# First round of a routed expert layer: W1 products by 128-token tiles, transposes by row halves, search copies later

## The chip, the cores and the metric

The kernel runs on one core of a Trainium2 chip. The metric is the device time of one execution in microseconds (us). Engines are named as in the profile: PE is TensorE's matmul, PEld its weight load, DVE is VectorE, ACT is ScalarE, POOL is GpSimd, SP is SyncE. "L1369" is line 1369 of the kernel.

## What is computed

The first part is windowed attention over 8 batches of 8 heads, 576 positions and 64 columns; its rows become `x`, 4608 tokens of 512 columns. The second part routes the tokens to 8 experts and is where the change lies:

```python
logits = x @ w_gate
order = np.argsort(-logits.flatten())
for idx in order:
    tok, e = (int(idx) // E, int(idx) % E)
    if assigned[tok] >= 0 or counts[e] >= cap:   # cap = 4608 / 8 = 576
        continue
    assigned[tok] = e
    counts[e] += 1
for e in range(E):
    mask = assigned == e
    h = np.maximum(x[mask] @ w1[e], 0.0)
    out[mask] = h @ w2[e]
```

Each expert takes 576 tokens; `w1[e]` is 512 x 1024 and `w2[e]` is 1024 x 512.

## The kernel before, in words

Attention (L273 to L720) writes its rows to `xd` in device memory and leaves the gate's logits on the chip. The experts are then filled one after the other in eight rounds; a round is one expert. `R.alone()` (L858) searches the threshold of the first full expert with nothing beside it, and its list of tokens is made by `settle` (L1219) and `listing` (L1250).

**A round's data.** `gather` (L1276) fetches the 576 token rows with five indirect DMAs (L1283, POOL), four tiles of 128 tokens and one of 64 (`MSZ`). PE turns them (transposes against an identity), ACT rounds the turned rows to `XH` (type float32r, L1149 through `act`) and DVE keeps the rest in `XL` (L1150 through `sub`), both in `split` (L1309). In the first round (r = 0) `gather` itself turns one tile at a time, four transposes of 128 x 128 for a tile, into a bank of `PYR` (two banks, `py`) or `PTR` (one, `ptx`) (L1296 to L1305). In later rounds `turn_halves` (L1317) turns all five tiles in one go, each by its two 64-row halves, into `PHR`'s banks (`ph`, L1338).

**A round's products.** `expert` (L1352) has eight blocks f of 128 hidden columns. `first(f, j)` (L1356) makes block f for half j of the tokens: j = 0 is columns 0 to 256 (tiles 0 and 1), j = 1 is columns 256 to 576 (tiles 2, 3 and 4). Each is 12 products (L1369): four row blocks d, times w1h with XH, w1l with XH, and w1h with XL. The stationary operand is a 128 x 128 block of weights, the moving one 256 or 320 token columns. The result goes through ACT (relu to `hb`) and DVE (the rest, L1389), and then its bank is free; `PHR[j]` has two banks for each j. The order of (f, j) is (0,0), (1,0), (0,1), (1,1), (2,0), (2,1), and so on; `gemm` (L1348) makes each group of products depend on the one before it, so that order is fixed. W2's products follow (L1411, L1414, L1416), then rows go out by indirect DMA (L1437).

**The search for the next expert** runs beside the products: `close`, `leave` and `start` on DVE, then `copies` on ACT (L854, `ohr`, the flags repeated for PE), then eight steps of `counts` on PE (nine small products, L724) and `step` on DVE (L761 to L771, L738).

**What sets the order.** [...] A planner written in the kernel, `Schedule` (L156), simulates all engines with a cost in ns for each operation and due times (the longest remaining path, less a boost), and emits the instructions of each engine in that order. The planner takes a product of n columns to cost n/2.4 + 13.5 ns (L1381), and a turn of the first round 460 ns. Where the plan leaves PE idle ahead of a turn, it puts in products of zeros into the bank `PHR[0].tiles[1]` (`keep_clock`, L120) to hold the clock. [...]

Of the kernel before, what the change touches and what calls it, by code (L numbers as in the profile page):

```python
# [1116 lines left out]
def moe(tc, ctx, C, R, xd, w1, w2, out):  # L1117
# [35 lines left out]
    def weights(n, r, f, deps):  # L1153

        raw, old, use = RAW[n].take()
        if n == "1" and r < len(AHEAD_W) and f == AHEAD_W[r]:

            gate[r] = op("POOL", 100, lambda: nc.gpsimd.memset(raw[:1, :1], 0.0), [got[r, 1], *old], B_G)
        later = None
        if r in gate:  # L1160
            deps = [*deps, gate[r]]
            later = X[r][-2][0] if n == "1" and r else None

        def load():
            if n == "1":
                src = w1[bass.ds(E[r], 1), f].rearrange("o p d f -> p (o d f)")
            else:
                src = w2[bass.ds(E[r], 1), f * 128:f * 128 + 128, :].rearrange("o p d -> p (o d)")
            nc.sync.dma_start(raw, src)

        ld = op("SP", 60, load, [*deps, *old], dma=T_W)
        h, oldh, useh = WH[n].take()
        l, oldl, usel = WL[n].take()
        hi = op("ACT", 525, lambda: act(h, raw), [ld, *oldh, st["row"] if n == "1" and r == 0 else None, later], B_W)
        if (n, r) in ADDED:
            use.append(hi)
            ne = op("ACT", 525, lambda: nc.scalar.activation(l, h.bitcast(F32), AF.Copy, scale=-1.0), [hi, *oldl], B_W)
            useh.append(ne)
            lo = op("POOL", 1040, lambda: nc.gpsimd.dma_start(l, raw, accum_op=OP.add), [ne], B_W, lat=T_A if (n, r) != ADDED[2] else 500,
                    dma=T_AM if (n, r) != ADDED[2] else T_GM)  # L1180
            use.append(lo)
        else:
            lo = op("DVE", 600, lambda: sub(nc.vector, l, raw, h), [ld, hi, *oldl, st["ix"] if n == "1" and r == 0 else None], B_W)
            use += [hi, lo]
        useh.append(lo)
        return h, l, hi, lo, useh, usel
# [32 lines left out]
    def settle(r, e):  # L1219

        if r == 0:
            rk = nd = None
        elif r < NE - 1:
            nd = st["need"] = chain("DVE", 1180, R.members, [e], B_L)
            rk = chain("PE", 70, R.ranks, [nd], B_L)
        else:
            nd = chain("DVE", 400, R.rest, [e, st["left"], st["slots"]], B_L)
            rk = chain("PE", 70, R.ranks, [nd], B_L)

        def accept():  # L1230
            if r:
                R.before()
            R.accept()

        ac = chain("DVE", 730 if r else 200, accept, [rk, nd], B_L)
        sl = st["slots"] = chain("DVE", 400, lambda: R.slots(r == 0), [ac, st.get("digits")], B_L)
        ix, box = listing(r, sl)
        st["ix"] = ix
        st["left"] = None
        if r == NE - 2:  # L1240
            st["left"] = chain("DVE", 400, R.assign, [ac])
        elif r < NE - 1:
            cl = chain("DVE", 1780, R.close, [nd, ix if r == 0 else None])
            lv = chain("DVE", 1050, R.leave, [cl, ac])
            oc = chain("ACT", 1055, lambda: R.copies(R.oh, nc.scalar), [lv])
            gf = chain("DVE", 670, R.start, [cl])
            st["next"] = [oc, gf]
        return ix, box

    def listing(r, sl):  # L1250
# [25 lines left out]
    def gather(r, ix, box):  # L1276

        done, gs = [], []
        for m, n in enumerate(MSZ):
            xg, old, use = XG.take()  # L1280

            def get(xg=xg, n=n, m=m):
                nc.gpsimd.indirect_dma_start(out=xg[:n], out_offset=None, in_=xd,  # L1283
                                             in_offset=bass.IndirectOffsetOnAxis(ap=box[0][:n, m:m + 1], axis=0))

            g = op("POOL", 1040 if r else 1500, get, [ix, *old], B_G,
                   lat=2500 if r <= DENSE else T_GL if r == NE - 2 else T_G, dma=T_GM if 0 < r <= DENSE else 0)
            got[r, m] = g
            gs.append((g, xg, use))
        if r:  # L1290
            turn_halves(r, gs, done)
            return done
        for m, n in enumerate(MSZ):
            g, xg, use = gs[m]
            pt, old, usep = (PYR if m % 3 < 2 else PTR).take()
            pt = pt.rearrange("p (d x) -> p d x", d=ND)[:, :, :n]  # L1296

            def turn(pt=pt, xg=xg, n=n):
                for d in range(ND):
                    nc.tensor.transpose(pt[:, d], xg[:n, 128 * d:128 * d + 128], C["identf"][:n, :n])  # L1300

            t = op("PE", 460 if n == 128 else 250, turn, [g, *old], B_TR)
            use.append(t)
            turns.append(t)
            at = slice(128 * m, 128 * m + n)  # L1305
            split(r, m, n, t, pt, XH[:, :, at], XL[:, :, at], usep, done)
        return done

    def split(r, m, n, t, pt, a, b, use, done):  # L1309
        full = 500 if n == 128 else 290  # L1310
        wx = x_users.get((r - 1, 0 if m < 2 else 1), [])
        s0 = op("ACT", full, lambda: act(a, pt), [t, *wx], B_TR)
        s1 = op("DVE", full + 100, lambda: sub(nc.vector, b, pt, a), [s0], B_TR)
        use += [s0, s1]
        done.append((s0, s1))

    def turn_halves(r, gs, done):  # L1317

# [29 lines left out]
    def gemm(cost, fn, deps):  # L1348
        last[0] = op("PE", cost, fn, [*deps, last[0]])
        return last[0]  # L1350

    def expert(r, X, box, W1, W2):  # L1352

        hidden = {}

        def first(f, j):  # L1356
            ph, old, use = PHR[j].take()
            h, l, hi, lo, useh, usel = W1[f]
            c0, c1 = CUT[j:j + 2]
            o = ph[:, :c1 - c0]  # L1360
            xs = X[:2] if j == 0 else X[2:]
            pairs = [(d, i) for d in range(ND) for i in range(3)]
            if f < 2:
                pairs = [(d, i) for i in range(3) for d in range(ND)]

            def mm(ps_):
                for d, i in ps_:
                    a, b = ((h, XH), (l, XH), (h, XL))[i]
                    nc.tensor.matmul(o, a[:, d * 128:d * 128 + 128], b[:, d, c0:c1],  # L1369
                                     start=((d, i) == pairs[0]), stop=((d, i) == pairs[-1]))  # L1370

            n = ND if f < 2 else 3
            for k in range(0, 3 * ND, n):
                part = pairs[k:k + n]
                deps = [hi, *old] if k == 0 else []
                if any(i == 1 for _, i in part):
                    deps.append(lo)
                deps += [x[0] for x in xs] if k == 0 else []
                if any(i == 2 for _, i in part):
                    deps += [x[1] for x in xs]  # L1380
                g = gemm(n * ((c1 - c0) / 2.4 + 13.5), lambda part=part: mm(part), deps)  # L1381
            useh.append(g)
            usel.append(g)
            x_users.setdefault((r, j), []).append(g)
            if j == 0:
                hidden[f] = [*HB.take(), []]
            hb, oldh, useb, done = hidden[f]
            hh = op("ACT", 270 if j == 0 else 320, lambda: act(hb[:, c0:c1], o, AF.Relu), [g, *(oldh if j == 0 else ())], B_H)
            hl = op("DVE", 335 if j == 0 else 400, lambda: nc.vector.scalar_tensor_tensor(  # L1389
                hb[:, CAP + c0:CAP + c1], o, 0.0, hb[:, c0:c1], op0=OP.max, op1=OP.subtract), [hh], B_HL)  # L1390
            use += [hh, hl]
            done.append(hl)
            if j == 1:
                h2 = op("ACT", 190, lambda: act(hb[:, 2 * CAP:], o[:, c1 - c0 - 64:], AF.Relu), [g], B_H)
                use.append(h2)
                done.append(h2)

        for f, j in ((0, 0), (1, 0), (0, 1), (1, 1), *((f, j) for f in range(2, NF) for j in range(2))):
            first(f, j)
        gemm1_end[r] = last[0]  # L1400
        for m, n in sorted(enumerate(MSZ), key=lambda x: x[1] if r == NE - 1 else 0):
# [50 lines left out]
    def round_(r):  # L1452
        e = None
        if r:
            e = search(r) if r < NE - 1 else chain("DVE", 650, R.last, [st["fetch"], st["need"]])
        en = st["fetch"] = EN[r] = op("SP", 100, lambda: fetch(r, R.eidx), [e])
        ix, BOX[r] = settle(r, e)
        toks[r] = st["tok"]
        X[r] = gather(r, ix, BOX[r])
        W[r] = [weights("1", r, f, [en]) for f in range(NF)]  # L1460

    def first_gather():
# [92 lines left out]
```

## Time and profile before

| | |
|---|---|
| Time, median of 3 runs | 631.48 us (631.08 to 631.92) |
| The profiled execution's own time | 631.08 us |
| Its span in the profile | 629.2 us |
| PE busy | 604.9 us (96%) |
| PEld busy | 529.0 us (84%) |
| DVE, ACT, POOL busy | 443.6, 304.1, 197.4 us |
| First gather's turn of the first round begins | 174.60 us |
| First product of the first round begins | 177.48 us |

A PE busy share says that some matmul was in flight, not that the array was full; the ends of matmuls are modelled. The pace of a stream of products is read better from when they start. Weight loads run beside the products, one ahead.

### The profile page before, as it was taken

How to read it: one execution, taken by the hardware profiler on the slowest of the kernel's cores; microseconds unless marked ns; L12 is line 12 of the kernel's file. 1: busy time of each engine (PE TensorE's matmuls, PEld its weight loads, DVE VectorE, ACT ScalarE, POOL GpSimd, SP SyncE). 2: the span in 40 equal slices, each digit the busy share in tenths (PEclk: the TensorE clock that was granted, in tenths of full speed). 3: DMA queues.
4: the chain of work that ended last, by engine and by line, in shares of the span. 5: the costliest groups of instructions: out<-in, count | busy, mean ns of one | idle time of the engine just before them, and what ended most of it. 6: DMA issues, size and time to landing. Idle time of an engine off the chain costs nothing.

```text
span 629.2 us, 17943 instructions
## 1 busy us (share of the span) xinstructions
PE 604.9 (96%) x6749; PEld 529.0 (84%) x6750; DVE 443.6 (71%) x1896; ACT 304.1 (48%) x695; POOL 197.4 (31%) x331
## 2 busy tenths in 40 slices
PE   8999999896599999999999999999999999999996
PEld 5888888786379879978998898799889879988985
DVE  4778879777887878777986988698889826714200
ACT  4787788671167238744252434435343345324211
POOL 3643434330253175352025104300610520341011
PEclk9999999997599999999999999999999999999999
DMA  8989999852187279972073136116423744122001
GB/s 313 394 252 300 287 269 316 279 119 60 55 272 154 84 164 288 239 241 85 9 253 109 59 106 220 68 28 211 133 76 102 246 161 147 40 71 76 1 26 51
DMA packets 62679, 100.11 MB, mean 159 GB/s; under 512 B 7280, under 2 KB 26224, under 8 KB 62592
## 3 DMA queue, kind: packets, MB, share of 16 engines
q1 hardware_dynamic: 53216, 73.75, 36.2%
q0 software_dynamic: 9376, 25.21, 15.4%
q8 instruction: 53, 0.87, 0.6%
q14 instruction: 34, 0.28, 0.1%
HBM read 73.77 MB, written 18.87 MB: 147 GB/s over the span
## 4 chain that ended last, share of the span: by engine, by line
PE 59%; issue 12%; DVE 7%; POOL 3%; DMA 1%; POOLq 0%; ACT 0%; SPq 0%; DVEq 0%
PE ph L1369 26%; PE py L1411 19%; PE pz L724 2%; PE py L1414 2%; PE py L1416 2%; PE px L426 1%; POOL out L1437 1%; PE px L418 1%; PE ph L1338 1%; DVE ob L1072 1%; PE pm L400 1%; POOL xg L1283 1%; PE pz L798 1%; DMA raw<-in_moe_w 1%; PE px L477 1%
## 5 line engine op out<-in xcount | busy, mean ns | idle before, releaser
L1411 PE MATMUL py<-w2h,hb 128*128 128x512 f32 x512 | 165.0, 394 | 0.0
L1369 PE MATMUL ph<-xh,w1h 128*128 128x256 f32 (+1 forms) x512 | 138.4, 301 | 0.0
L1369 PE MATMUL ph<-xh,w1l 128*128 128x256 f32 (+1 forms) x512 | 136.6, 297 | 0.0
L1369 PE MATMUL ph<-xl,w1h 128*128 128x256 f32 (+1 forms) x512 | 135.9, 296 | 0.0
L1411 PEld LDWEIGHTS py<-w2h,hb 128*128 128x128 f32 x512 | 96.1, 188 | 19.7
L1149 ACT ACTIVATE hb<-ph 128x256 fp32r<-128x256 f32 (+2 forms) x192 | 59.7, 346 | 100.9 <-PE ph L1369 99.1
L1411 PE MATMUL py<-w2l,hb 128*128 128x512 f32 x256 | 99.8, 390 | 0.0
L1369 PEld LDWEIGHTS ph<-xh,w1h 128*128 128x128 f32 x512 | 91.8, 190 | 0.7
L1369 PEld LDWEIGHTS ph<-xl,w1h 128*128 128x128 f32 x512 | 91.6, 189 | 0.1
L1369 PEld LDWEIGHTS ph<-xh,w1l 128*128 128x128 f32 x512 | 91.5, 190 | 0.0
L1437 POOL DMA_INDIRECT out<-y,tok x40 | 40.6, 1015 | 144.6 <-ACT y L1149 65.3
L1149 ACT ACTIVATE y<-py 128x512 f32<-128x512 f32 (+1 forms) x40 | 23.9, 596 | 121.0 <-PE py L1411 85.7
L411 POOL TENSOR_TENSOR sc<-sc,mx 128x480 f32<-128x480 f32 x64 | 56.9, 909 | 78.4 <-DVE mx L405 78.3
L1389 DVE SCALAR_TENSOR_TENSOR hb<-ph,hb 128x320 fp32r<-128x320 f32 (+1 forms) x128 | 57.3, 452 | 33.1 <-ACT hb L1149 32.0
L405 DVE CUSTOM_DVE_ANT_0 sc<-pm,const 128x96 f32<-128x96 f32 x288 | 53.6, 252 | 17.6 <-PE pm L400 17.3
L1283 POOL DMA_INDIRECT xg<-xd,idx x40 | 41.6, 1039 | 55.8 <-issue 38.0
L1411 PEld LDWEIGHTS py<-w2l,hb 128*128 128x128 f32 x256 | 48.1, 188 | 9.1
L1150 DVE TENSOR_TENSOR w2l<-raw,w2h 128x512 fp32r<-128x512 f32 x48 | 31.9, 685 | 20.4 <-ACT w2h L1149 20.1
L414 ACT ACTIVATE et<-px 96x384 f32<-96x384 f32 x96 | 40.2, 488 | 12.5 <-PE px L418 10.4
L1149 ACT ACTIVATE w1h<-raw 128x512 fp32r<-128x512 f32 x64 | 37.8, 628 | 9.3 <-DMA raw<-in_moe_w 9.2
L418 PE MATMUL px<-const,sc 128*96 128x128 f32 x288 | 38.6, 277 | 2.2 <-issue 1.5
L1149 ACT ACTIVATE w2h<-raw 128x512 fp32r<-128x512 f32 x64 | 36.8, 622 | 3.0 <-DMA raw<-in_moe_w 3.0
(206 smaller groups left out, 967.6 us busy)
## 6 DMA issues: line engine op xcount, KB each, us to landing
raw<-in_moe_w SPq DMA_DIRECT2D x128, 256.0 KB, 4.0
k<-in_kp SPq DMA_DIRECT2D x16, 304.0 KB, 5.8
k<-in_kd SPq DMA_DIRECT2D x16, 304.0 KB, 6.8
q<-in_qp SPq DMA_DIRECT2D x16, 288.0 KB, 5.7
q<-in_qd SPq DMA_DIRECT2D x16, 288.0 KB, 6.6
xd<-xs SPq DMA_DIRECT2D x64, 72.0 KB, 2.8
xd<-xs SPq DMA_DIRECT2D x16, 288.0 KB, 5.6
w2l<-raw POOLq DMA_DIRECT2D x16, 256.0 KB
```

The lines of the kernel that those rows point to most:

```text
L405: nc.vector.tensor_tensor_reduce(out=sc[:, c], in0=pms[g][:, c // 2 * KB:c // 2 * KB + KB], in1=mm[:, c if self.kind else min(1, c)], scal ...
L411: nc.gpsimd.tensor_tensor(sc[:, g::2], sc[:, g::2], mx[:, g::2, None].to_broadcast([128, n, KB]), op=OP.subtract)
L414: nc.scalar.activation(self.E0[:, 384 * j:384 * j + 384], pt[:KB, :384], AF.Exp, scale=-1.0)
L418: nc.tensor.transpose(pt[:KB, 128 * x:128 * x + 128], sc[:, ORD[3 * j + x]], C["identf"])
L724: nc.tensor.matmul(o, self.ohr[:, j].rearrange("p r x -> p (r x)"), self.G[:, 4 * j:4 * j + 4, :w], start=(j == 0), stop=(j == NCH // 4 - 1))
L1149: act = lambda o, i, f=AF.Copy: nc.scalar.activation(o, i, f)
L1150: sub = lambda e, o, a, b: e.tensor_tensor(o, a, b, op=OP.subtract)
L1283: nc.gpsimd.indirect_dma_start(out=xg[:n], out_offset=None, in_=xd, in_offset=bass.IndirectOffsetOnAxis(ap=box[0][:n, m:m + 1], axis=0))
L1369: nc.tensor.matmul(o, a[:, d * 128:d * 128 + 128], b[:, d, c0:c1], start=((d, i) == pairs[0]), stop=((d, i) == pairs[-1]))
L1389: hl = op("DVE", 335 if j == 0 else 400, lambda: nc.vector.scalar_tensor_tensor(hb[:, CAP + c0:CAP + c1], o, 0.0, hb[:, c0:c1], op0=OP.max ...
L1411: nc.tensor.matmul(py, x, w, start=(f + i == 0), stop=(f == NF - 1 and i == 2))
L1437: s = nc.gpsimd.indirect_dma_start(out=out, out_offset=bass.IndirectOffsetOnAxis(ap=box[1][:n, m:m + 1], axis=0), in_=y[:n], in_offset=None)
```

## The change

It does three things, all in the first round (r = 0).

First, `first` is split into `products` (one group of products of block f, a range of token columns), `keep` (what follows once a bank is complete) and `by_tile`. In the first round the blocks f = 0 and f = 1 of half j = 0 are made by `by_tile`: for tile 0 and then for tile 1, the three kinds of product for f = 0 and f = 1 in turn, each a group of four products with 128 moving columns. The order then goes on with (2,0), (0,1), (1,1), (2,1).

Second, the turning of the first round moves to `turn_each`: a tile of 128 tokens is turned by its two 64-row halves into two banks (`PHR[1]` for odd tiles, `PYR` for even ones), each half split on its own; the fifth tile uses `PTR`. The planner's costs are 300 for such a turn and 330 for a half's split.

Third, `copies` of the first search waits for tile 1's two roundings.

```diff
-            oc = chain("ACT", 1055, lambda: R.copies(R.oh, nc.scalar), [lv])
+            if r == 0:
+                st["leave"] = lv
+            else:
+                oc = chain("ACT", 1055, lambda: R.copies(R.oh, nc.scalar), [lv])
             gf = chain("DVE", 670, R.start, [cl])
-            st["next"] = [oc, gf]
+            st["next"] = [oc, gf] if r else [gf]
...
+    def turn_each(r, gs, done):
         for m, n in enumerate(MSZ):
             g, xg, use = gs[m]
-            pt, old, usep = (PYR if m % 3 < 2 else PTR).take()
-            pt = pt.rearrange("p (d x) -> p d x", d=ND)[:, :, :n]
+            ring_ = PHR[1] if m % 2 else PYR
+            got_ = [ring_.take() for _ in range(2)] if n == 128 else [PTR.take()]
+            old = [y for x in got_ for y in x[1]]
+            halves = [x[0][:, :64 * ND].rearrange("p (d y) -> p d y", d=ND) for x in got_]
...
                 for d in range(ND):
-                    nc.tensor.transpose(pt[:, d], xg[:n, 128 * d:128 * d + 128], C["identf"][:n, :n])
-            t = op("PE", 460 if n == 128 else 250, turn, [g, *old], B_TR)
+                    for h, o in enumerate(halves):
+                        p = slice(64 * h, 64 * h + 64)
+                        nc.tensor.transpose(o[:, d], xg[p, 128 * d:128 * d + 128], C["identf"][p, p])
+            t = op("PE", 300, turn, [g, *old, *turns[-1:]], B_TR)
...
+            for h, (o, x) in enumerate(zip(halves, got_)):
+                p = slice(at.start + 64 * h, at.start + 64 * h + 64)
+                split(r, m, 64, t, o, XH[:, :, p], XL[:, :, p], x[2], parts)
...
-        full = 500 if n == 128 else 290
+        full = 500 if n == 128 else 290 if r or m == 4 else 330
...
+        def products(f, j, c0, c1, xs, part, open_):
...
+            return gemm(len(part) * ((c1 - c0) / 2.4 + 13.5), mm, deps)
...
+        def by_tile():
+            for m in range(2):
+                for i in range(3):
+                    for f in range(2):
+                        g = products(f, 0, 128 * m, 128 * m + 128, X[m:m + 1], [(d, i) for d in range(ND)], (i == 0, i == 2))
+                        if m and i == 2:
+                            keep(f, 0, g)
...
-        for f, j in ((0, 0), (1, 0), (0, 1), (1, 1), *((f, j) for f in range(2, NF) for j in range(2))):
+        if r == 0:
+            by_tile()
+            order = [(2, 0), (0, 1), (1, 1), (2, 1)]
+        else:
+            order = [(0, 0), (1, 0), (0, 1), (1, 1), (2, 0), (2, 1)]
+        for f, j in order + [(f, j) for f in range(3, NF) for j in range(2)]:
             first(f, j)
...
+        if r == 0:
+            st["next"].insert(0, chain("ACT", 1055, lambda: R.copies(R.oh, nc.scalar), [st["leave"], *X[r][1][0]]))
```

## Rows read from the trace of the kernel before

**Rows 1.** Busy us per engine from 182.2 to 624 us; then granted clock, DMA share, GB/s

```profile
182.20:624.00 441.80, 440.61 (x3221) 391.36 (x3217) 306.27 (x987) 187.78 (x426) 126.98 (x230) 1.00 0.42 127
```

**Rows 2.** The same by stretches of 10 us: PE, PEld, DVE, ACT, POOL

```profile
170.00:180.00 10.00, 8.84 (x51) 5.13 (x51) 8.54 (x27) 3.79 (x7) 7.40 (x14) 0.84 0.55 161
180.00:190.00 10.00, 10.00 (x82) 9.70 (x81) 8.84 (x25) 7.84 (x20) 2.88 (x7) 1.00 0.97 299
```

**Rows 3.** Timeline of PE alone, two later stalls: start, us, ..., [idle before]

```profile
226.14 0.45 PE L724 MATMUL pz<-G,ohr 128*128 128x64 bf16 x9 [0.24 <-DVE G L736]
...
268.63 0.24 PE L1079 MATMUL ptx<-rx,ob 128*128 128x40 bf16 x3 [0.62 <-DVE ob L1072]
```

**Rows 4.** Timeline of the first round's start: start, us, engine, line, [idle before]

```profile
172.40 0.95 POOL L1283 DMA_INDIRECT xg<-xd,idx  x1 [0.30 <-issue]
...
174.60 0.66 PE L1300 MATMUL py<-const,xg 128*128 128x128 f32 x4 [0.48 <-DMA xg<-xd,idx]
...
175.30 0.60 ACT L1149 ACTIVATE xh<-py 128x512 fp32r<-128x512 f32 x1 [3.75 <-PE py L1300]
175.79 1.16 ACT L854 ACTIVATE ohr<-oh 128x1152 bf16<-128x1152 bf16 x1
...
176.00 0.66 PE L1300 MATMUL py<-const,xg 128*128 128x128 f32 x4 [0.30 <-DMA xg<-xd,idx]
...
177.00 0.46 PE L724 MATMUL pz<-G,ohr 128*128 128x64 bf16 x9 [0.35 <-DVE xl L1150]
...
177.48 0.74 PE L1369 MATMUL ph<-xh,w1h 128*128 128x256 f32 x4
...
180.99 0.32 PEld L1300 LDWEIGHTS py<-const,xg 64*128 64x128 f32 x4 [0.19 <-DMA xg<-xd,idx]
...
181.38 0.53 PEld L1369 LDWEIGHTS ph<-xl,w1h 128*128 128x128 f32 x4
...
182.23 0.59 PEld L1369 LDWEIGHTS ph<-xh,w1h 128*128 128x128 f32 x4
...
182.57 0.42 DVE L1389 SCALAR_TENSOR_TENSOR hb<-ph,hb 128x256 fp32r<-128x256 f32 x1 [0.24 <-ACT hb L1149]
```

**Rows 5.** Chain that ended last, 165 to 240 us: start, us on the chain, what

```profile
178.66 0.96 PE ph L1369 x8
...
193.85 0.30 PE pz L724 x9
...
235.01 1.13 PE ph L1338 x32
```

**Rows 6.** Timeline, two groups of four 320-column products (two more lie between)

```profile
182.92 0.75 PE L1369 MATMUL ph<-xh,w1l 128*128 128x320 f32 x4
...
184.68 0.75 PE L1369 MATMUL ph<-xh,w1l 128*128 128x320 f32 x4
```

**Rows 7.** Weight loads by line and form: xcount | busy us, mean ns | idle before

```profile
L1369 PEld LDWEIGHTS ph<-xl,w1h 128*128 128x128 f32 x512 | 91.6, 189 | 0.1
...
L710 PEld LDWEIGHTS px<-cc,const 128*128 128x128 f32 x2 | 0.3, 188 | 0.0
```

**Rows 8.** Timeline of weight loads alone, narrow windows holding two loads each

```profile
148.27 0.30 PEld L710 LDWEIGHTS px<-cc,const 128*128 128x128 f32 x2
...
181.38 0.30 PEld L1369 LDWEIGHTS ph<-xl,w1h 128*128 128x128 f32 x2
```

**Rows 9.** ACT and DVE copies by line and form, 165 to 190 us

```profile
L1150 DVE TENSOR_TENSOR xl<-py,xh 128x512 fp32r<-128x512 f32 x3 | 2.1, 687 | 0.9 <-ACT xh L1149 0.8
...
L1150 DVE TENSOR_TENSOR xl<-py,xh 128x256 fp32r<-128x256 f32 x1 | 0.4, 425 | 0.1
...
L1149 ACT ACTIVATE xh<-py 128x256 fp32r<-128x256 f32 x1 | 0.4, 387 | 0.8 <-DVE xl L1150 0.8
```

**Rows 10.** Timeline: the first search's third step on DVE; the second round's last gather

```profile
187.47 0.23 DVE L754 TENSOR_SCALAR kb<-kv,base 128x16 f32<-128x16 f32 x1
...
231.12 0.91 POOL L1283 DMA_INDIRECT xg<-xd,idx  x1 [0.30 <-issue]
```

More of the change, by code (lines that the diff above doesn't have):

```diff
@@ L1161, in weights @@
             deps = [*deps, gate[r]]
-            later = X[r][-2][0] if n == "1" and r else None
+            later = X[r][-2][0][0] if n == "1" and r else None
         def load():
@@ L1289, in gather, with turn @@
             gs.append((g, xg, use))
-        if r:
-            turn_halves(r, gs, done)
-            return done
+        (turn_halves if r else turn_each)(r, gs, done)
+        return done
+    def turn_each(r, gs, done):
         for m, n in enumerate(MSZ):
             g, xg, use = gs[m]
-            pt, old, usep = (PYR if m % 3 < 2 else PTR).take()
-            pt = pt.rearrange("p (d x) -> p d x", d=ND)[:, :, :n]
-            def turn(pt=pt, xg=xg, n=n):
+            ring_ = PHR[1] if m % 2 else PYR
+            got_ = [ring_.take() for _ in range(2)] if n == 128 else [PTR.take()]
+            old = [y for x in got_ for y in x[1]]
+            halves = [x[0][:, :64 * ND].rearrange("p (d y) -> p d y", d=ND) for x in got_]
+            def turn(halves=halves, xg=xg):
                 for d in range(ND):
-                    nc.tensor.transpose(pt[:, d], xg[:n, 128 * d:128 * d + 128], C["identf"][:n, :n])
-            t = op("PE", 460 if n == 128 else 250, turn, [g, *old], B_TR)
+                    for h, o in enumerate(halves):
+                        p = slice(64 * h, 64 * h + 64)
+                        nc.tensor.transpose(o[:, d], xg[p, 128 * d:128 * d + 128], C["identf"][p, p])
+            t = op("PE", 300, turn, [g, *old, *turns[-1:]], B_TR)
             use.append(t)
@@ L1305, in gather @@
             at = slice(128 * m, 128 * m + n)
-            split(r, m, n, t, pt, XH[:, :, at], XL[:, :, at], usep, done)
-        return done
+            parts = []
+            for h, (o, x) in enumerate(zip(halves, got_)):
+                p = slice(at.start + 64 * h, at.start + 64 * h + 64)
+                split(r, m, 64, t, o, XH[:, :, p], XL[:, :, p], x[2], parts)
+            done.append(([x for x, _ in parts], [x for _, x in parts]))
     def split(r, m, n, t, pt, a, b, use, done):
-        full = 500 if n == 128 else 290
+        full = 500 if n == 128 else 290 if r or m == 4 else 330
         wx = x_users.get((r - 1, 0 if m < 2 else 1), [])
@@ L1314, in split @@
         use += [s0, s1]
-        done.append((s0, s1))
+        done.append(([s0], [s1]) if r else (s0, s1))
     def turn_halves(r, gs, done):
@@ L1354, in expert, with mm @@
         hidden = {}
+        banks = {}
+        def products(f, j, c0, c1, xs, part, open_):
+            if (f, j) not in banks:
+                banks[f, j] = PHR[j].take()
+            ph, old, use = banks[f, j]
+            h, l, hi, lo, useh, usel = W1[f]
+            o = ph[:, c0 - CUT[j]:c1 - CUT[j]]
+            def mm():
+                for k, (d, i) in enumerate(part):
+                    a, b = ((h, XH), (l, XH), (h, XL))[i]
+                    nc.tensor.matmul(o, a[:, d * 128:d * 128 + 128], b[:, d, c0:c1],
+                                     start=open_[0] and k == 0, stop=open_[1] and k == len(part) - 1)
+            deps = [hi, *old] if open_[0] else []
+            if any(i == 1 for _, i in part):
+                deps.append(lo)
+            deps += [z for x in xs for z in x[0]] if open_[0] else []
+            if any(i == 2 for _, i in part):
+                deps += [z for x in xs for z in x[1]]
+            return gemm(len(part) * ((c1 - c0) / 2.4 + 13.5), mm, deps)
         def first(f, j):
-            ph, old, use = PHR[j].take()
-            h, l, hi, lo, useh, usel = W1[f]
             c0, c1 = CUT[j:j + 2]
-            o = ph[:, :c1 - c0]
             xs = X[:2] if j == 0 else X[2:]
@@ L1364, in first, with keep @@
                 pairs = [(d, i) for i in range(3) for d in range(ND)]
[L1366 to L1370, printed above, removed]
             n = ND if f < 2 else 3
             for k in range(0, 3 * ND, n):
[L1374 to L1381, printed above, removed]
+                g = products(f, j, c0, c1, xs, pairs[k:k + n], (k == 0, k + n == 3 * ND))
+            keep(f, j, g)
+        def by_tile():
[5 more added lines that the diff above has]
+                            keep(f, 0, g)
+        def keep(f, j, g):
+            ph, _, use = banks[f, j]
+            _, _, _, _, useh, usel = W1[f]
+            c0, c1 = CUT[j:j + 2]
+            o = ph[:, :c1 - c0]
             useh.append(g)
```

## The prediction

> **What bounds the kernel now.** I read the busy time by stretches first, then the timeline of the first round's start, then the chain that ended last. [...]
>
> The start is bound by the gathers and then by PE. Tile 0 is turned at 174.60, tile 1 at 176.00; each turn takes 0.66 us with its tail; ACT then needs 0.6 us for a tile. The first products begin at 177.48, when tile 1 too is rounded. `ohr`'s copy lies between the two roundings, and the search's first counts fill part of PE's wait at 177.00. From 177.48 PE has no hole of note, and the first product of (0,1) is issued at 182.23 [rows 4].
>
> **The price on which all hangs: a product with 128 moving columns.** The trace has none in float32r. Two things can set the pace. One is the moving operand. Products of 256 columns come every 0.96/8 = 0.120 us [rows 5], those of 320 every (184.68 - 182.92)/12 = 0.147 us [rows 6]; the slope is 0.42 ns a column, so 128 columns alone would come every 0.067 us, which is also what the planner charges. The other is the weight load, since every product has a new 128 x 128 block. A load lasts 0.189 us [rows 7], and two of them, the second right behind the first, last 0.30 us together; so the second starts 0.11 us after the first, and a stream of loads can't come faster [rows 8]. The same 0.11 us stands between L710's two loads, whose products move 16 columns only: there no moving operand can be what holds them apart [rows 7, 8]. With 256 columns the two limits coincide, which is why the weight load doesn't show in this kernel; halve the columns and it is what remains. I take 0.113 us, between the load's 0.11 and the 0.120 that a 256-column product takes; the ends for the range are 0.067 and 0.120.
>
> [...]
>
> **The sum, from 175.90 to the same point of the work.** Before, the stretch from 175.90 to 182.23 is 6.33 us [rows 4]. It holds 24 products, four turns (tiles 1 to 4), two counts and about 1.1 us in which PE has nothing to do.
>
> After, the first product can be issued at 175.9. Tile 0 by halves is eight transposes at 1.13/32 = 0.035 us [rows 5], 0.28 us, with a tail of 0.22 us (0.66 less four at 0.11) [rows 4]; from 175.10 ACT rounds two halves at 0.387 us each [rows 9], to 175.9. From there PE has in a row:
> - 48 products at 0.113: 5.42 us (24 at 0.120, 2.88 us, before).
> - tiles 1, 2 and 3 by halves, 3 x 0.28 = 0.84 us (0.44 each before).
> - the fifth tile, as before, 0.39 us, from 180.99 to 181.38 [rows 4].
> - two counts at 0.30 us [rows 5]: 0.60 us. The first lay in a wait of PE and cost nothing; that cover is gone.
> - a wait that the new order makes. (2,0) is the third taker of `PHR[0]`'s two banks, and now follows at once. A bank is free when ACT and DVE have been over it: from the first load of a block's last group at 181.38 to DVE's end at 182.99 is 1.61 us [rows 4]. Behind f = 0's last group there is only that of f = 1, so two groups of 0.45 us; 0.7 us are left, of which the fifth tile's turn fills 0.39. Some 0.3 us stay open (none if the second counts fall in there). Every later product is queued behind (2,0).
>
> 5.42 + 0.84 + 0.39 + 0.60 + 0.3 = 7.55 us, against 6.33: **1.2 us slower**. With 0.110 and no open wait it is 0.8 us, with 0.120 it is 1.6 us.
>
> **What lies beside.** ACT gets two copies of 0.387 for one of 0.594, about 0.2 us more for each of four tiles; DVE two of 0.425 for one of 0.687 [rows 9], the same. The six product groups of tile 0 cover it: tile 1 is fully split by about 178.5, and its first product is not due before 178.9. If that cover went (at 0.067 a product), PE would wait about 0.2 us. The two products of zeros ahead of tile 1's turn go, since the plan now has a product there; PE then stands idle for 0.8 us. Holes of 0.48 us at 174.1 and 0.35 at 176.65 are there now [rows 4], and the clock stays at the full level from 174 on; I take no fall, though 0.8 is longer than either. No DMA is moved: the gathers' issues on POOL and the weights' on SP keep their places. (2,0) needs its W1 block some 2.5 us sooner; I take it as there, and what it would cost if not lies inside the range.
>
> **The search** starts later. `ohr` waits for tile 1's second half: that is turned by 176.85 (a group from 175.90 to 176.35, 0.28 and the tail of 0.22), plus 2 x 0.387 is 177.65, plus 1.16 is 178.8, so the first counts move from 177.00 to 178.8 or later, and all steps on DVE behind them. I cost this at nothing: DVE was through with the third step's flags at 187.70 [rows 10], and the third counts stand in PE's queue at 193.85 [rows 5], where the due times put them. 6 us of slack take up 1.8. What it costs without that cover is a rival.
>
> A measurement of this kernel can tell about 0.2% from no change, 1.26 us. The profiled execution took 631.08 us (span 629.2), 0.4 under the median of 631.48. On its own time the sum gives 632.3; on the median **632.7**, at the upper edge of what counts as no change.
>
> **Rivals.**
>
> *The search is late at the border of the rounds.* The second round's rows are gathered up to 232.03 [rows 10] and, if they land as in the first round (2.65 us from the end of the issue at 173.35 to 176.00 [rows 4]), are there at 234.7; the turn stands at 235.0 [rows 5]. So 0.3 us of slack. If the planner keeps less of the 6 us than I think and the list of tokens comes 1.8 us later against the products, PE waits up to 1.5 us there: 631.48 + 1.2 + 1.5 = 634.2. It decides as soon as the delay that is left at the last step passes 0.3 us. For it: DVE is the second busiest engine, with 8.84 of 10 us in 180 to 190 [rows 2]. Against it: the slack at 193.85, and that PE, too, is later by 1.2 us. Chance 0.22, all of it slower.
>
> *The moving operand sets the pace.* If a load can run further ahead than the row shows, a product costs 0.067 us: 3.2 for 5.42. The order's wait then is longer (two groups are 0.54 of 1.61 us, and the fifth tile lands at 180.99 whatever PE does), so (2,0) begins at about 181.4 with the second counts to come, 181.7 against 182.23: 0.5 us faster, 631.0. [...] Speaking for it: 320 and 256 columns follow one line. Against it: the spacing of loads. Chance 0.12, of which 0.02 faster and 0.10 within.
>
> *The plan comes out better later.* The planner places everything anew. If the stalls of 0.24 and 0.62 go as well, 0.9 us come back, and with the cheap product 1.4 us in all: 630.1. Chance 0.08, of which 0.06 faster.
>
> That the products don't start early at all (the plan puts tile 1's turn ahead of tile 0's first group) would change little: PE is then held from 176.0, not 175.9, and the sum moves by 0.1 us.
>
> **The numbers.** The forecast, 1.2 us slower and the rest shifted with it, has 0.58; its own range is 632.2 to 633.2, which the limit of 632.74 cuts: 0.37 within, 0.21 slower. Faster 0.06 + 0.02 = 0.08; within 0.37 + 0.10 + 0.02 = 0.49; slower 0.21 + 0.22 = 0.43. The range reaches from just under the cheap product's time, 630.7, to the late search's, 634.2.
>
> **What will show it.** Right: weight loads of 128-column products 0.11 us or more apart; the first of them at about 175.9; (2,0) at 183.2 or so and held by DVE's `hb`; PE with no hole at 235 to 240. Wrong: 0.07 to 0.08 us apart; (2,0) before 182; a PE wait for a gather at the second round's turn; a granted clock under 1.00 between 175 and 183, which would make every term longer.

## The result, and the profile after

The changed kernel took 638.66 us in the median of 12 runs (632.99 to 645.90), the kernel before 631.61 beside it (629.83 to 633.33). The ratio is 1.0089, with a 95% interval of 1.0066 to 1.0112: slower by 0.9%, some 5.6 us, where 1.2 us were forecast. The ratio leaves out the two slowest executions of the changed kernel, 643.28 and 645.90; the medians of all lie 7.1 us apart. The time lies above the stated range.

The runs of the changed kernel fall into two groups, by TensorE's mean granted clock over the run: four with 0.98 took 633 to 637 us, eight with 0.97 or less took 637.6 to 645.9. So there are two costs to be found, one of every run and one of those in which the clock fell.

The profile after is of a run in which it fell. The windows of that trace, PE alone; the columns are stretch, its length, PE busy, granted clock, DMA share, GB/s:

```profile
174.60:181.00 6.40, 5.39 (x29) 0.50 0.48 156
181.20:184.50 3.30, 2.53 (x28) 1.00 0.74 195
184.60:198.20 13.60, 13.60 (x81) 0.50 0.69 230
198.30:205.00 6.70, 6.70 (x56) 1.00 0.47 80
```

The granted clock is 0.50, the half level, while products of zeros run; it is 1.00, the full level, from 181.2, before the first tile is turned at 181.6, and 0.50 again from 184.6 for 13.6 us, in the midst of the new products. In the kernel before it is 1.00 while the first round starts, and stays there [rows 1]. The window of before (PE, PEld, DVE, ACT, POOL, then clock, DMA share, GB/s):

```profile
174.00:183.20 9.20, 8.04 (x71) 6.76 (x71) 7.60 (x23) 5.14 (x10) 5.77 (x16) 1.00 0.80 245
```

This run's attention part, which the change leaves as it was, also had a fall to 0.50, at about 96 to 103 us; the first gather is issued at 177.82 here and at 170.75 in the profile of before. I therefore compare from that issue to the end: 458.5 us before (170.75 to 629.2), 466.1 here (177.82 to 643.9).

Weight loads of the same run at the half level (start, us, engine, line, what, count):

```profile
188.15 1.83 PEld L1380 LDWEIGHTS ph<-xh,w1h 128*128 128x128 f32 x8
189.86 1.83 PEld L1380 LDWEIGHTS ph<-xh,w1l 128*128 128x128 f32 x8
...
194.19 0.55 PEld L724 LDWEIGHTS <-ohr 128*128 128x128 bf16 x9
194.82 0.50 PEld L1309 LDWEIGHTS ptx<-const,xg 64*128 64x128 f32 x4
195.44 0.29 PEld L1380 LDWEIGHTS ph<-xh,w1h 128*128 128x128 f32 x1
```

Eight loads take 1.71 us here (188.15 to 189.86), 0.214 us each, nearly twice the 0.111 us of the full level (below). The first 256-column product comes at 195.44, and at this level these too come every 0.214 us (eleven from 195.82 to 197.96); the clock is at 1.00 again from 198.3. After that PE is as full as it was [rows 1], busy for 438.92 us of 440.10, so that at most 1.2 us of a loss at the start could be taken up there (PE, PEld, DVE, ACT, POOL, then clock, DMA share, GB/s):

```profile
198.30:638.40 440.10, 438.92 (x3211) 389.83 (x3210) 306.81 (x993) 186.60 (x423) 126.91 (x230) 1.00 0.41 123
```

### The profile page after: what moved, and what is told of

The parts are those of the page before. It is cut to its first block, busy times and chain, and to the rows that moved or that the text cites. A ratio compares the mean times of both kernels' runs of the same rounds, so it can differ in the third digit from the quotient of the medians.

```text
span 643.9 us, 18027 instructions
## 1 busy us (share of the span) xinstructions
PE 616.7 (96%) x6788; PEld 540.3 (84%) x6788; DVE 445.1 (69%) x1900; ACT 305.4 (47%) x699; POOL 196.9 (31%) x331
## 4 chain that ended last, share of the span: by engine, by line
PE 76%; issue 12%; DVE 6%; POOL 3%; DMA 1%; ACT 0%; POOLq 0%; SPq 0%
PE ph L1380 27%; PE py L1449 18%; PE px L426 6%; PE px L418 5%; PE pm L400 5%; PE px L477 3%; PE pz L724 2%; PE py L1452 2%; PE py L1454 2%; POOL out L1475 1%; PE px L534 1%; PE ph L1350 1%; DVE ob L1072 1%; DMA raw<-in_moe_w 1%; PE pz L798 1%
## 5 line engine op out<-in xcount | busy, mean ns | idle before, releaser
L1380 PE MATMUL ph<-xh,w1h 128*128 128x256 f32 (+2 forms) x520 | 140.9, 304 | 0.7 <-ACT xh L1149 0.7
L1380 PE MATMUL ph<-xh,w1l 128*128 128x256 f32 (+2 forms) x520 | 139.3, 301 | 0.0
L1380 PE MATMUL ph<-xl,w1h 128*128 128x256 f32 (+2 forms) x520 | 139.2, 301 | 0.0
L1149 ACT ACTIVATE hb<-ph 128x64 fp32r<-128x64 f32 (+2 forms) x192 | 59.9, 346 | 110.4 <-PE ph L1380 108.0
L1380 PEld LDWEIGHTS ph<-xh,w1h 128*128 128x128 f32 x520 | 94.2, 193 | 1.6 <-ACT xh L1149 0.9
L1380 PEld LDWEIGHTS ph<-xl,w1h 128*128 128x128 f32 x520 | 94.7, 195 | 0.2
L1380 PEld LDWEIGHTS ph<-xh,w1l 128*128 128x128 f32 x520 | 94.3, 194 | 0.0
L414 ACT ACTIVATE et<-px 96x384 f32<-96x384 f32 x96 | 40.4, 490 | 13.6 <-PE px L418 12.9
L400 PE MATMUL pm<-k,q 64*64 64x96 f32 x1152 | 36.3, 256 | 2.3 <-issue 1.7
```

Of the source, the lines that this page charges most:

```text
L400: nc.tensor.matmul(o[w:w + 64], self.Q[c][r:r + 64], self.K[c][r:r + 64], start=True, stop=True)
L414: nc.scalar.activation(self.E0[:, 384 * j:384 * j + 384], pt[:KB, :384], AF.Exp, scale=-1.0)
L1149: act = lambda o, i, f=AF.Copy: nc.scalar.activation(o, i, f)
```

## The experiments

Each run below is 12 executions, beside 29 to 35 of the kernel before on the same chip. "Low" counts executions with a mean granted clock of 0.974 or less; the kernel before had 0, 1, 0 and 1 of them in the four sets. The mean doesn't say where the clock fell, and a short fall can hide in it: the profiled execution of again fell for some 7 us, in the attention part alone, and has 0.976. Counts of 12 are small: 5 and 8 of 12, or 1 and 3, are not told apart by them. The ratio is to the kernel before.

| run | what it is | median us | before | low of 12 | ratio (95%) |
|---|---|---|---|---|---|
| again | the change | 640.00 | 631.88 | 8 | 1.0092 (1.0053 to 1.0132) |
| early | early copies | 638.34 | 631.88 | 8 | 1.0074 (1.0041 to 1.0106) |
| oldorder | (0,1), (1,1) ahead of (2,0) | 635.14 | 631.88 | 5 | 1.0048 (1.0015 to 1.0082) |
| whole | whole turns | 632.46 | 631.88 | 0 | 1.0018 (0.9995 to 1.0042) |
| tileonly | whole turns, early copies | 633.46 | 632.07 | 0 | 1.0029 (0.9999 to 1.0059) |
| zeros3 | three products of zeros | 633.04 | 632.07 | 0 | 1.0013 (0.9985 to 1.0041) |
| zeros1 | one product of zeros | 632.52 | 631.58 | 1 | 1.0011 (0.9982 to 1.0041) |
| t0whole | tile 0 whole | 634.41 | 631.58 | 5 | 1.0035 (0.9996 to 1.0073) |
| t01whole | tiles 0 and 1 whole | 633.13 | 631.05 | 0 | 1.0018 (0.9993 to 1.0043) |
| twice | tile 0's halves turned twice | 634.28 | 631.05 | 3 | 1.0041 (1.0006 to 1.0076) |
| wide | 256-column products | 632.47 | 632.07 | 1 | 1.0004 (0.9973 to 1.0035) |
| widenz | the same without zeros | 632.49 | 631.58 | 1 | 1.0007 (0.9979 to 1.0035) |
| wideold | halves and late copies alone | 631.80 | 631.58 | 0 | 0.9999 (0.9970 to 1.0028) |
| late | late copies alone | 631.93 | 631.05 | 0 | 0.9998 (0.9973 to 1.0023) |
| nozeros | before without the zeros | 631.27 | 632.07 | 0 | 0.9981 (0.9956 to 1.0005) |

### First set: products, hole or chance

**wide.** The 128-column products go, the rest stays:

```diff
-            by_tile()
+            first(0, 0)
+            first(1, 0)
```

> The change with the products of f = 0 and f = 1 put back to 256 columns; turns by halves, the later copies and the new order stay. Hole theory (the clock falls since PE now idles some 0.7 us behind tile 0's turn, where products of zeros stood): the plan has its zeros there again, so no fall; about 631.3 us. Stream theory (the clock falls since 128-column products leave the array waiting for weight loads for some 5 us): no fall either, 631.3. Chance theory (the falls have nothing to do with the change): some runs fall all the same, 631 and 637 mixed.

Measured: 632.47, one low run of 12, no difference from before (1.0004). One low run is no mixture as the first comparison had it, so the fall needs more than what is left here; hole and stream both stand.

**tileonly.** Products by tile and the new order, with `gather`'s old turns and `copies` back behind `leave`:

```diff
-            got_ = [ring_.take() for _ in range(2)] if n == 128 else [PTR.take()]
+            pt, old, usep = (PYR if m % 3 < 2 else PTR).take()
...
-            st["next"] = [oc, gf] if r else [gf]
+            st["next"] = [oc, gf]
```

> The change's products by tile and its order alone; turns whole as before, copies early as before. Hole and stream theories: the half level appears in the first round in most runs, 637 to 640 us. Chance theory: 632 to 633 in nearly all. The direct cost at the full clock should be that of the change plus 0.6 us for the dearer turns.

Measured: no low run, 633.46, ratio 1.0029. Neither hole nor stream foresaw this: the 128-column products don't bring the clock down by themselves, and the hole, which is nearly as long here (0.69 us, with the change 0.75), doesn't either. Whether the falls belonged to the first comparison's chip is open at this point.

**zeros3.** The hole behind tile 0's turn is filled:

```diff
             def turn(halves=halves, xg=xg):
...
+                if xg is gs[0][1]:
+                    keep_clock(nc, R.zero, fill, 3)
```

> The change with three products of zeros behind tile 0's turn, which fill the hole ahead of the first group. Hole theory: no fall, 633 us in all runs. Stream theory: the clock falls as often as with the change, most runs at 638 to 640. In both the full-clock runs are those of the change, 633 to 634, since the zeros end before the first group is ready.

Measured: no low run, 633.04, all but two between 630.95 and 633.77. The stream theory's fall doesn't come. Its timeline of PE shows what stands in the hole now:

```profile
174.79 0.46 PE L1309 MATMUL py<-const,xg 64*128 64x64 f32 x8
175.18 0.82 PE L120 MATMUL ph<-zero 128*128 128x512 bf16 x3
176.00 0.66 PE L1382 MATMUL ph<-xh,w1h 128*128 128x128 f32 x4
```

**nozeros.** The kernel before, without the two products of zeros ahead of tile 1's turn:

```diff
-        if x in turns:
+        if x in turns and x is not turns[1]:
```

> The kernel before without the two products of zeros ahead of tile 1's turn. Hole theory: the half level comes in some runs, which then take some 5 us more, 636 to 637. Stream theory: no fall, 631.5 like before.

Measured: no low run, 631.27. The hole theory as I had put it is wrong too: with whole turns, missing zeros cost nothing, though PE then waits 0.88 us ahead of tile 1's turn.

### Second set: which part of the change

**again.** The changed kernel unedited.

> The changed kernel itself, beside the kernel before and the variants below on one chip. If the fall of the clock in the first round belongs to the change, it shows here in most runs as in the first comparison, 637 to 640 us, and the runs without it take 633 to 634. If it belonged to the chip or the hour of the first comparison, it is rare here and the median is 633 to 634, 1.2 to 2 us over before.

Measured: 8 of 12 low, as in the first comparison; median 640.00. The other four took 632.37 to 638.25. The fall belongs to the change. This run's profile is of an execution that kept the clock in the first round (its 638.25 us hold the fall in the attention part), and serves below for the cost that every run pays. Its windows, PE alone:

```profile
178.80:190.00 11.20, 10.05 (x105) 1.00 0.81 246
190.00:200.00 10.00, 10.00 (x81) 1.00 0.86 223
```

**early.** `copies` back behind `leave`, the rest as changed:

```diff
-            if r == 0:
-                st["leave"] = lv
-            else:
+            if True:
                 oc = chain("ACT", 1055, lambda: R.copies(R.oh, nc.scalar), [lv])
...
-            st["next"] = [oc, gf] if r else [gf]
+            st["next"] = [oc, gf]
...
-        if r == 0:
-            st["next"].insert(0, chain("ACT", 1055, lambda: R.copies(R.oh, nc.scalar), [st["leave"], *X[r][1][0]]))
```

> The change with ohr's copy put back to where it was, behind the leave step on DVE; products by tile, turns by halves and order stay. If the later copies are worth something, this loses up to 0.5 us at the full clock (ACT rounds tile 1 later). Hole theory: the hole behind tile 0's turn stays, so the clock falls as often as with the change. If it falls less, the later counts have to do with it.

Measured: 8 of 12 low; the other four 631.1 to 636.3. The later copies are not what lets the clock fall. Its profile shows the fall in the same place (columns as above), and 465.8 us from the first gather's issue to the end (170.34 to 636.1):

```profile
174.40:177.60 3.20, 2.45 (x30) 1.00 0.69 204
177.80:191.30 13.50, 13.50 (x80) 0.50 0.67 223
191.40:200.00 8.60, 8.60 (x70) 1.00 0.55 105
```

**whole.** Whole turns, later copies, products by tile (the first lines of tileonly's edit).

> The change with turns of whole tiles, four transposes each; products by tile, later copies and order stay. By the rows of before it pays 3 x 0.16 us more on PE, so 0.5 us over the change at the full clock. Hole theory: as large a hole, so the clock falls as often as with the change; if the turns by halves are what lets it fall, it doesn't fall here.

Measured: no low run, 632.46. One part makes the difference between 8 and 0: the turns by halves, with which go the rounding of a tile in two pieces and the choice of banks. (Two executions, with 0.975 and 0.977, could hold a short fall.) And whole turns were not dearer at the full clock but, if anything, cheaper.

**oldorder.**

```diff
-            order = [(2, 0), (0, 1), (1, 1), (2, 1)]
+            order = [(0, 1), (1, 1), (2, 0), (2, 1)]
```

> The change with (0,1) and (1,1) put back ahead of (2,0). The wait for PHR's bank ahead of (2,0) goes: 0.3 us less than the change at the full clock if that wait is what I took it for, up to 0.7 if the fifth tile's turn doesn't fill it; a gain of nothing, or a loss, if (0,1) then waits for the fifth tile. The clock falls as often as with the change.

Measured: 5 of 12 low; the other seven have a median of 632.86. The clock falls without the new order too. What the order is worth can't be told from these: in its timeline (0,1) waits 0.47 us for the fifth tile's rounding, in place of (2,0).

```profile
182.29 0.46 PE L1309 MATMUL ptx<-const,xg 64*128 64x64 f32 x4
183.22 0.85 PE L1380 MATMUL ph<-xh,w1h 128*128 128x320 f32 x4 [0.47 <-ACT xh L1149]
```

### Third and fourth set: which turns, and with what

**zeros1.** As zeros3, with one product of zeros (`keep_clock(nc, R.zero, fill, 1)`).

> The change with one product of zeros behind tile 0's turn instead of none (three kept the clock in every run). If what PE does between the turn and the first group decides, one does part of it: falls in fewer runs than with the change, 632.5 to 633.5 in the others. If three did it by another way, such as moving the groups, one does nothing and most runs take 638 to 640.

Measured: one low run. A single product of zeros, some 0.2 us of PE (three take 0.82 us in zeros3, two 0.59 in the kernel before), does nearly what three do.

**widenz.** wide, with nozeros' edit.

> 256-column products, turns by halves, later copies, as in the run with wide products, but without the products of zeros ahead of tile 1's turn. If the short turn and the hole behind it decide, the clock falls here too in many runs, 636 to 639, with no 128-column product in the kernel. If the stream of 128-column products is needed for the fall, none: 632 to 632.5.

Measured: 632.49, one run at 640; eight of the other eleven have a mean clock of 0.975 to 0.977, where the kernel before mostly has 0.979 or more. The profile says why (PE, PEld, DVE, ACT and POOL by stretches):

```profile
171.70:175.00 3.30, 1.73 (x20) 0.84 (x18) 3.04 (x11) 0.72 (x3) 2.38 (x4) 1.00 0.71 205
175.10:181.80 6.70, 6.15 (x36) 5.47 (x37) 2.69 (x7) 3.25 (x8) 3.26 (x14) 0.50 0.85 255
181.90:190.00 8.10, 8.10 (x67) 7.79 (x66) 4.32 (x12) 6.82 (x16) 1.87 (x2) 1.00 0.80 232
```

The clock falls here too, with no 128-column product in the kernel, but comes back after 6.7 us instead of 13.6. The span from the first gather to the end, 169.16 to 630.1, is 460.9 us against 459.0 in wide (170.26 to 629.3): by these two profiles the fall costs some 2 us here, a third of what it costs the change (5.9, below). The medians don't bear out as much: widenz lies 0.9 us over its kernel before, wide 0.4 over its own. So a fall needs no 128-column product; while those ran, it lasted twice as long, in two profiles against one. (That the same products at another place would hold the clock down wasn't tried. Nor were whole turns with these holes: PE waits 1.03 and 0.74 us here, 0.88 and 0.20 in nozeros.)

**wideold.** The edits of wide and of oldorder.

> Only the turns by halves and the later copies of the change: 256-column products in the old order, with the plan's zeros. No fall. The cheaper turns give up to 0.6 us on PE where nothing else waits: 631.3 to 632.0, beside 632 for the kernel before; no wait of (2,0) for a bank.

Measured: 0.9999 of before, no low run. The turns by halves and the later copies give no gain.

**t0whole.** Tile 0 alone takes one bank and four transposes:

```diff
+            cut = 64 if n == 64 or not (m == 0) else 128
...
-                        p = slice(64 * h, 64 * h + 64)
+                        p = slice(cut * h, cut * h + cut)
```

> The change with tile 0 alone turned whole (four transposes, one bank, one split), the other tiles by halves, products by tile. If the stretch from the zeros to the first group decides, the clock stays as with whole turns, 632.5 to 633.5. If the turns by halves inside the stream of products are what lets it fall, it falls as with the change, 638 to 640 in most runs.

Measured: 5 of 12 low, 636.8 to 640.5, the others 631.0 to 634.7. Between the two answers. Tile 0's turn by halves isn't needed for a fall; whether it has a part in it can't be told from 5 of 12 against the change's 16 of 24.

**t01whole.** The same with `m < 2`.

> The change with tiles 0 and 1 turned whole, tiles 2 and 3 by halves. With tile 0 alone whole, 5 runs of 12 lost the clock; with all whole none. If the early part decides, tile 1's turn among it, none or one falls here, 632.5 to 633.5. If every turn by halves takes its part, some 3 to 5 of 12 still fall.

Measured: no low run, against t0whole's 5, from which it differs in tile 1's turn and rounding alone. The early part decides: with tiles 0 and 1 whole, halves for the later ones do no harm. The banks are the change's own here (one of the two for a whole tile), so the old banks are not what kept the clock in whole.

**twice.** Tile 0's turn by halves, its transposes issued twice:

```diff
-                for d in range(ND):
+                for d in [*range(ND), *(range(ND) if xg is gs[0][1] else ())]:
```

> The change with tile 0's turn by halves done twice over, sixteen transposes for eight, so that PE is at work longer between the zeros and the first group though on 64 rows at a time. If it is the time without work that lets the clock fall, this keeps it as one product of zeros did: 633 to 634 in nearly all runs. If transposes by halves don't hold the clock however many there are, it falls as with the change, 638 to 641 in most runs.

Measured: 3 of 12 low. Less than with the change (16 of 24 in its two sets), not clearly more than with products of zeros (1 of 24 in zeros1 and zeros3). So more work in that place helps. The hole stays (0.74 us), and the falls are about as frequent as with tile 0 whole (t0whole, 5 of 12); whether transposes on 64 rows hold the clock less well than a product of zeros can't be told from these counts. A sharper line between kind and amount of work is not drawn by these runs.

**late.** wideold with whole turns.

> Only the later copies of the change: whole turns, 256-column products in the old order, the plan's zeros. Tile 1 is rounded 0.14 us sooner and the first counts come some 1.5 us later with 6 us of slack behind them: 0 to 0.3 us faster than the kernel before, no fall of the clock. If the change holds a gain at all, it is here.

Measured: 0.9998 of before. No part of the change that was run by itself gains, and no version here beats the kernel before beyond its interval. (The products by tile were run only with the new order or with the turns by halves.)

## Why the prediction was wrong

**Where it failed: the clock.** The step was "I take no fall, though 0.8 is longer than either". The prediction saw that the zeros ahead of tile 1's turn would go, compared the hole with the shorter ones in the trace, and costed it at nothing; it gave no rival for it, only a clause among the signs of error. The fall came in 16 of 24 executions of the change. Its price, by the two profiles: from the first gather to the end 466.1 us with the fall (the first profile) and 460.2 without (again, 176.23 to 636.4), 5.9 us. One product of zeros in the hole takes it away, but for one low run in 12. The hole alone didn't do it (nozeros and whole, no low run in 12 each), which I had also got wrong in the first set of experiments; it takes the hole together with early turns by halves, of which tile 1's is enough (t0whole, by its mean clocks). Tile 0's alone wasn't tried. Why such turns let the clock go stays open, and so does why 8 of the 24 kept it. In the two profiled falls of 13.6 us the clock had risen 0.4 us (after) and 0.0 us (early) ahead of tile 0's turn; in two profiles with the same stretch and no fall it had risen 1.2 us (again) and 2.5 us (oldorder) ahead. So it may go with when the clock rose, which four profiles don't show (widenz, with other holes, fell at 1.3).

**The sum at the full clock was near, with one term wrong and one beside it.** From the first gather to the end, again takes 460.2 us against 458.5: 1.7 us slower where the sum said 1.2. Such a difference of two profiles is good to about 1 us: nozeros, which is before without two products of zeros, has 459.4 (173.53 to 632.9). The eight executions of both sets with a mean clock over 0.974 have a median of 633.5, 1.6 to 1.9 over before. Weight loads of again at the full level:

```profile
179.98 0.32 PEld L1309 LDWEIGHTS py<-const,xg 64*128 64x128 f32 x8 [0.90 <-DMA xg<-xd,idx]
181.18 0.52 PEld L1380 LDWEIGHTS ph<-xh,w1h 128*128 128x128 f32 x4 [0.88 <-ACT xh L1149]
...
183.50 0.53 PEld L1380 LDWEIGHTS ph<-xl,w1h 128*128 128x128 f32 x4
184.10 0.33 PEld L1309 LDWEIGHTS py<-const,xg 64*128 64x128 f32 x8
184.49 0.52 PEld L1380 LDWEIGHTS ph<-xl,w1h 128*128 128x128 f32 x4
184.94 0.97 PEld L1380 LDWEIGHTS ph<-xh,w1h 128*128 128x128 f32 x8
185.83 0.97 PEld L1380 LDWEIGHTS ph<-xh,w1l 128*128 128x128 f32 x8
...
188.22 0.34 PEld L724 LDWEIGHTS <-ohr 128*128 128x128 bf16 x9
188.61 0.32 PEld L1309 LDWEIGHTS ptx<-const,xg 64*128 64x128 f32 x4
189.00 0.19 PEld L1380 LDWEIGHTS ph<-xh,w1h 128*128 128x128 f32 x1
```

- *The product's price, 0.113 us: right.* Eight take 185.83 - 184.94 = 0.89 us, 0.111 each. That is the loads' own spacing of 0.11 us [rows 8]: the weight load sets the pace, and the rival in which the moving operand does, at 0.067, is refuted.
- *The first group: 0.1 us early.* It starts 1.20 us after tile 0's turn does, where the sum had 1.30: ACT's two halves overlap (0.66 us for both, 180.47 to 181.13, for twice 0.387).
- *The turn by halves, 0.28 us: wrong, it is 0.54.* This is the term of the sum that was mis-sized. Four products from 183.50 on fill the loads' path to 183.94 (4 x 0.111); the next product's load comes at 184.49, behind the turn. I had taken the pace inside `turn_halves`, where 32 stand together [rows 5], and not what it takes to get in and out of a stream of full-height products. In the run whole the same place takes 0.42 us (its first group and (2,0) are shown too):

```profile
174.99 0.52 PEld L1374 LDWEIGHTS ph<-xh,w1h 128*128 128x128 f32 x4 [0.93 <-ACT xh L1149]
...
177.18 0.53 PEld L1374 LDWEIGHTS ph<-xl,w1h 128*128 128x128 f32 x4
177.66 0.42 PEld L1305 LDWEIGHTS ptx<-const,xg 128*128 128x128 f32 x4
178.04 0.53 PEld L1374 LDWEIGHTS ph<-xl,w1h 128*128 128x128 f32 x4
...
182.43 0.19 PEld L1374 LDWEIGHTS ph<-xh,w1h 128*128 128x128 f32 x1
```

  177.18 plus 0.44 is 177.62, the next at 178.04. So halves are dearer by 0.12 us a turn, three turns 0.4 us. That is what the same work shows: from the first group to (2,0) whole takes 7.44 us (174.99 to 182.43), again 7.82 (181.18 to 189.00). By the sum's terms, with the one count that comes ahead of (2,0), it is 7.25 (5.42 + 0.84 + 0.39 + 0.30 + 0.3). Three turns at 0.54 add 0.8 us to the sum.
- *The wait of (2,0) for a bank, 0.3 us: covered.* The first counts (188.22) and the fifth tile's turn (188.61) lie in it, and (2,0) starts right behind at 189.00. With 0.8 more for the turns, 0.3 less here and 0.1 less each for the first group and the products, 1.2 becomes 1.5, near the 1.7 measured. That the sum as it stood came near is in part luck: the mis-sized turns and the wait that didn't come have opposite signs.

**The late search: right that it costs nothing, wrong on when.** The first counts come 12.0 us after the first gather's issue, 5.7 later than before (6.25), not 1.8: the planner put them behind the whole of `by_tile`. Yet the third counts and the second round's turn in again's chain are shifted with the rest:

```profile
200.98 0.30 PE pz L724 x9
...
242.30 1.14 PE ph L1350 x32
```

From the first gather's issue that is 24.7 and 66.1 us, in before 23.1 and 64.3 [rows 5]: 1.6 and 1.8 later, no more than everything else, and PE has no wait at the turn. The 6 us of slack were there, and the rival of the late search didn't come. Neither did a better plan later: the stalls of PE [rows 3] stand again, 0.25 and 0.58 us.

## What to carry to other kernels

Halving the moving columns of products whose stationary block changes each time saved next to nothing on each here, since the weight load was then the limit (0.111 us for 128 columns, 0.120 for 256), and there were twice as many: find the load's spacing in the trace where two loads stand back to back. Where a plan fills PE's holes with products of zeros, a change that removes a hole from the plan but not from the chip takes the filling with it; count what held the clock as a part of what is removed, and give its fall a price of its own (5.9 us here, by two profiles). Transposes by row halves were cheap beside others of their kind (32 at 0.035 us each) and dear in the midst of full-height products (0.54 us for eight).

## What was not expected of the hardware

Early turns by 64-row halves with a hole of 0.75 us behind the first brought the clock to the half level in 16 of 24 executions; with tiles 0 and 1 turned at full height and a hole of 0.69 us, in none of 36 (whole, tileonly, t01whole; all by the mean clock of the run). Why is not settled by these runs: full-height turns are transposes too, and with tiles 0 and 1 so turned no run was low, while doubling tile 0's half-height ones left fewer falls than the change has (3 of 12). At the half level a float32r load of 128 columns took 0.214 us instead of 0.111, as long as a 256-column product took there, so the stream of 128-column products, bound by its loads, was slowed by a factor of 1.93; while it ran the clock stayed down for 13.6 us in two profiles (after, early), under 256-column products for 6.7 us in one (widenz).
